# Two layers of grouped-query decode attention: a limit of four loads in flight

## The chip, the cores and the metric

The kernel runs on one core of a Trainium2 chip. The metric is the device time of one execution in microseconds (us). Before the change it is 1258.97 us, the median of three runs (1254.94 to 1260.19).

## What is computed

The input x is a batch of 8 single tokens of width 512. It goes twice through the same two blocks, with the same weights and the same caches: an attention block with 32 query heads, 8 key/value heads and 8192 cached positions of width 128, and a dense block of width 1792. Cut to what matters:

```
def attention(x, k_cache, v_cache, wq, wo):      # caches: 8 x 8 x 8192 x 128, bf16
    q = (x @ wq) as 32 heads of 128              # 4 query heads share one k/v head
    scores = q . k * 128**-0.5
    o = softmax(scores) . v
    return o @ wo

def dense(x, w1, w2):
    return silu(x @ w1) @ w2

x = x + attention(layernorm(x), k_cache, v_cache, wq, wo)
x = x + dense(layernorm(x), w1, w2)
x = x + attention(layernorm(x), k_cache, v_cache, wq, wo)
x = x + dense(layernorm(x), w1, w2)
```

The caches hold 128 MiB each, and nothing that large stays on the core, so most of them is read twice, once for each layer.

## The kernel before

**Tiles.** A task is one layer, one batch element and one key/value head; there are 2 x 8 x 8 = 128. The K and the V of a task are each cut into four granules of 2048 positions, 512 KB, 128 partitions of 4 KB. A granule is one load and fills one slot of an SBUF arena; there are 27 slots (`NSLOT`). For each task PE transposes K in groups of eight blocks of 128 x 128 (`emit_t`, L390 to L407: matmuls against an identity into the PSUM bank TPp, copied back over the K granule by DVE, or by ACT for three of eight). It then makes the scores (`emit_s`, L421 to L437, bank SCp), and fourteen groups later the product with V (`emit_pv`, L468 to L483, bank OTp). In between stand the softmax's maximum, exponential and sum (L442 to L466, on DVE, ACT and POOL).

**Order of the tasks.** The K granules of the last 18 of 32 places of a batch element (`KEEP`) stay transposed in the arena from layer 0 to layer 1, so that they are loaded once; for these layer 1 loads only V. While they are held, 9 slots are left for the stream. `make_tasks` (L136) therefore puts, for each batch element, the kept tasks of layer 0, then tasks that load both K and V, and then the kept tasks of layer 1; beside them runs the chain from layer 0's attention to layer 1's queries (projection, residual, layer norm, dense block: `block_stages`, `query`, lines 495 to 638, matmuls L547 and L565). This repeats for the eight batch elements.

**The loads.** `plan_loads` (L167) sorts all 880 granule loads by the position at which they are needed, and gives each a slot and the position after which it is free. All loads are issued from SP's queue, by the helper `dma` (L313), in that one order; SP does nothing else but issue loads, and at the end the output. The first entries are x (8 KB), four K granules, wq (4 MB), more granules until the 27 slots are taken, then wo (4 MB), w1 and w2 (1.8 MB each). Every slot has a semaphore of its own (`slsem`), which a load raises by 16 when it has landed in full; the weights and x have theirs. Before SP issues a load into a slot it waits for those who last used the slot: PE's, DVE's and ACT's semaphores (`acquire`, L88, and `wait`, L79, which emits a wait at L85 only if this engine has not yet waited for as much). Nothing else holds a load back in the program. Other engines wait for a load only when they use it.

**Waits.** `op` (L304) does the same for every instruction of the engines, so that a group of eight matmuls (`mm_group`, L322) waits once, ahead of its first, and has no wait inside.

Of the kernel before, what the change touches and what calls it, by code (L numbers as in the profile page):

```python
# [26 lines left out]
CW = 32  # L27
SETTLE = 2
ACT_EVAC = (1, 4, 7)

BF16 = mybir.dt.bfloat16
FP32 = mybir.dt.float32
# [156 lines left out]
def bass_interleave_layers__gqa_block_cached__dense_activation_silu__decode_kernel(  # L189
    nc: bass.Bass,  # L190
    A_x: bass.AP,
    A_k_cache: bass.AP,
    A_v_cache: bass.AP,
    A_wq: bass.AP,
    A_wo: bass.AP,
    B_x: bass.AP,
    B_w1: bass.AP,
    B_w2: bass.AP,
    out: bass.AP,
):  # L200
    with ExitStack() as ctx:
        _build(ctx, nc, A_x, A_k_cache, A_v_cache, A_wq, A_wo, B_w1, B_w2, out)


def _build(ctx, nc, A_x, A_k_cache, A_v_cache, A_wq, A_wo, B_w1, B_w2, out):
# [43 lines left out]
    def half(slot, h):  # L249
        o = slot * SLOT + h * GRP * 128  # L250
        return ARENA[:, o:o + GRP * 128]
# [37 lines left out]
    syn = Sync(nc, ctx)  # L289
# [6 lines left out]
    def res(name):  # L296
        if name not in R:
            R[name] = Res(name)
        return R[name]

    def r_half(slot, h):
        return res(f"slot{slot}_{h}")

    def op(eng, inst_fn, reads=(), writes=()):  # L304
        reads = [res(n) if isinstance(n, str) else n for n in reads]
        writes = [res(n) if isinstance(n, str) else n for n in writes]
        syn.acquire(eng, reads, writes)
        inst = inst_fn()
        tok = syn.mark(inst, eng)
        syn.release(tok, reads, writes)  # L310
        return tok

    def dma(eng, out_ap, in_ap, counter, reads=(), writes=()):  # L313
        reads = [res(n) if isinstance(n, str) else n for n in reads]
        writes = [res(n) if isinstance(n, str) else n for n in writes]
        syn.acquire(eng, reads, writes)
        tok = counter.next_tok()
        eng.dma_start(out_ap, in_ap).then_inc(counter.sem, 16)  # L318
        syn.release(tok, reads, writes)
        return tok  # L320

    def mm_group(steps, reads=(), writes=()):  # L322
# [13 lines left out]
    def issue(d):  # L336
        cache = A_k_cache if d.kind == "K" else A_v_cache
        src = cache[d.b, d.g].rearrange("(k p c) d -> k p (c d)", k=NGRAN, p=128)[d.k]
        dst = ARENA[:, d.slot * SLOT:(d.slot + 1) * SLOT]
        dma(sp, dst, src, slsem[d.slot], writes=[r_half(d.slot, 0), r_half(d.slot, 1)])  # L340
        (k_slot if d.kind == "K" else v_slot)[(d.b, d.g, d.k)] = d.slot

    with nc.Block() as block:

        @block.sync
        def _(sync_eng):
            dma(sp, Xr[0:B, :], x_in, wsem["x"], writes=["Xr"])

            op(pool, lambda: pool.memset(ident[:, :], 1.0), writes=["ident"])
# [14 lines left out]
            def load_wq():  # L364
                dma(sp, wq_sb[:, :, :], A_wq.rearrange("(kt p) n -> p kt n", p=128), wsem["wq"], writes=["wq"])
# [24 lines left out]
            def emit_t(i):  # L390
# [12 lines left out]
                dst = half(slot, h)  # L403
                if n % 8 in ACT_EVAC:
                    op(act, lambda: act.copy(dst, TPp[tb][:, :]), reads=[f"TP{tb}"], writes=[r_half(slot, h)])  # L405
# [359 lines left out]
```

## Time and profile before

| | |
|---|---|
| median of three runs | 1258.97 us |
| the profiled execution | 1258.23 us, its span 1256.5 us |
| mean granted TensorE clock | 0.934 |
| bytes moved by DMA | 477.16 MB, mean 380 GB/s |
| PE matmuls | 935.6 us busy, 74% |
| V loads, issue to landing | 512 of 512 KB, median 10.3 us |
| K loads, issue to landing | 368 of 512 KB, median 12.0 us |

A profile describes one execution. The span runs from the first to the last instruction; the time is a little longer. "Busy" counts an engine's instructions; issues and waits of a queue are not busy. PE, PEld, DVE, ACT and POOL are engines, SPq is the queue from which the loads are issued, L433 is line 433 of the kernel. A wait row names who waited, for whom, and then us in total, number of times and the longest; "issue" there means that the engine waited for nothing that the profile shows. GB/s in the page is given for 40 equal slices of the span. In-flight counts in the text are loads that have been issued and have not landed, taken from the records of issues and landings in the trace.

### The profile page before, as it was taken

To read this page: it belongs to the slowest core of one execution; us is meant where nothing else is said; L and a number is where in the kernel's file an instruction comes from. 1 tells how busy PE (TensorE), PEld (TensorE's weight loads), DVE (VectorE), ACT (ScalarE), POOL (GpSimd) and SP (SyncE) were. 2 spreads that over 40 slices of the span, in tenths; PEclk is the share of its full clock that TensorE was granted. 3 is DMA by queue.
4 is the path that set the end of the run, shared out by engine and by line. 5 is a ranking of instruction groups with operands and counts; after the bars stand their busy time and mean duration, and the time that the engine had idled before them with its cause. 6 is when DMAs were issued, how large, how long until landed. Compare 5 with 4: busy or idle time off the path is not lost. (4 is left out here: it accounts for less than half of the span.)

```text
span 1256.5 us, 57306 instructions
## 1 busy us (share of the span) xinstructions
PE 935.6 (74%) x25592; PEld 905.4 (72%) x25592; DVE 459.9 (37%) x1334; ACT 480.8 (38%) x1310; POOL 117.7 (9%) x298
## 2 busy tenths in 40 slices
PE   3687777777777767888778776888678777777775
PEld 3677776777677767777777776877677777777775
DVE  2333441445234432444144432434134432344422
ACT  1344433444244433444344433443344433543431
POOL 0000111001100011001100111011100111000010
PEclk9889998999899998999898999899899988999986
DMA  9999999999999999999999999999999999999993
GB/s 372 385 398 407 388 362 408 407 394 375 372 407 389 398 349 408 407 360 366 396 408 366 392 332 407 408 363 367 389 408 367 396 355 407 407 395 354 380 408 134
DMA packets 133973, 477.16 MB, mean 380 GB/s; under 512 B 14160, under 2 KB 20064, under 8 KB 133216
## 3 DMA queue, kind: packets, MB, share of 16 engines
q1 hardware_dynamic: 133728, 473.51, 96.5%
q8 instruction: 201, 3.29, 1.1%
q14 instruction: 44, 0.36, 0.1%
HBM read 473.44 MB, written 0.01 MB: 377 GB/s over the span
## 5 line engine op out<-in xcount | busy, mean ns | idle before, releaser
L399 PE MATMUL TPp<-ident,arena 128*128 128x128 bf16 x5888 | 476.9, 226 | 123.7 <-DMA arena<-in_A_k_cache_dram 60.7
L407 DVE COPY arena<-TPp 128x1024 bf16<-128x1024 bf16 x460 | 317.2, 691 | 521.7 <-PE TPp L399 518.5
L433 PE MATMUL SCp<-QT,arena 128*128 128x48 bf16 x8192 | 407.5, 190 | 100.0 <-issue 98.5
L405 ACT COPY arena<-TPp 128x1024 bf16<-128x1024 bf16 x276 | 278.9, 1011 | 523.1 <-PE TPp L399 523.0
L399 PEld LDWEIGHTS TPp<-ident,arena 128*128 128x128 bf16 x5888 | 356.2, 101 | 135.2 <-DMA arena<-in_A_k_cache_dram 71.6
L478 PE MATMUL OTp<-PT,arena 128*128 128x48 bf16 x8192 | 390.7, 187 | 52.2 <-issue 43.0
L433 PEld LDWEIGHTS SCp<-QT,arena 128*128 128x128 bf16 x8192 | 330.4, 100 | 115.3 <-issue 113.5
L478 PEld LDWEIGHTS OTp<-PT,arena 128*128 128x128 bf16 x8192 | 297.6, 99 | 55.0 <-issue 46.9
L454 ACT ACTIVATE PT<-SCp,nb 128x64 bf16<-128x64 f32 x512 | 161.1, 315 | 219.7 <-PE OTp L478 77.9
L446 POOL PARTITION_ALL_REDUCE mxa<-mx x128 | 47.5, 371 | 718.4 <-DVE mx L444 695.9
L454 ACT ACTIVATION_READ_ACCUMULATOR PT<-SCp,nb 128x1 f32 x512 | 99.0, 193 | 0.0
L461 POOL PARTITION_ALL_REDUCE ssa<-rs x128 | 55.2, 432 | 345.8 <-ACT PT L454 345.8
L492 DVE TENSOR_TENSOR at<-OTp,rcp 128x4 bf16<-128x4 f32 x128 | 20.7, 162 | 120.0 <-PE OTp L478 120.0
L444 DVE TENSOR_REDUCE mx<-SCp 128x4 f32<-128x256 f32 x128 | 52.6, 411 | 32.7 <-PE SCp L433 32.7
L565 PE MATMUL MISC<-at,wo 128*128 128x32 bf16 (+1 forms) x1152 | 39.5, 176 | 10.9 <-DMA wo<-in_A_wo_dram 5.5
L547 PE MATMUL MISC<-xnT,wq 128*128 128x32 bf16 (+1 forms) x1152 | 35.0, 177 | 8.5 <-issue 7.2
L565 PEld LDWEIGHTS MISC<-at,wo 128*128 128x128 bf16 x1152 | 33.9, 96 | 9.5 <-DMA wo<-in_A_wo_dram 5.6
L547 PEld LDWEIGHTS MISC<-xnT,wq 128*128 128x128 bf16 x1152 | 31.9, 96 | 9.2 <-issue 7.6
L451 DVE TENSOR_SCALAR nb<-mxa 128x4 f32<-128x4 f32 x128 | 21.4, 167 | 40.9 <-POOL mxa L446 40.9
L466 DVE RECIPROCAL rcp<-ssa 128x4 f32<-128x4 f32 x128 | 21.6, 169 | 7.6 <-POOL ssa L461 7.6
L547 PE MATMUL MISC<-hsT,w 128*128 128x32 bf16 (+1 forms) x504 | 16.3, 177 | 6.8 <-issue 4.9
L547 PE MATMUL MISC<-xnT,w 128*128 128x32 bf16 (+1 forms) x504 | 15.4, 176 | 6.5 <-DVE xnT L534 4.9
(34 smaller groups left out, 110.2 us busy)
## 6 DMA issues: line engine op xcount, KB each, us to landing
arena<-in_A_v_cache_dram SPq DMA_DIRECT2D x512, 512.0 KB, 10.3
arena<-in_A_k_cache_dram SPq DMA_DIRECT2D x368, 512.0 KB, 12.0
wq<-in_A_wq_dram SPq DMA_DIRECT2D x1, 4096.0 KB, 16.4
wo<-in_A_wo_dram SPq DMA_DIRECT2D x1, 4096.0 KB, 25.9
w<-in_B_w_dram SPq DMA_DIRECT2D x2, 1792.0 KB, 22.7
Xr<-in_A_x_dram SPq DMA_DIRECT2D x1, 8.0 KB
out_dram<-Xr SPq DMA_DIRECT2D x1, 8.0 KB
```

What stands on the lines that cost most here:

```text
L399: lambda c=c: pe.transpose(tpv[:, c, :], chunk(slot, h * GRP + c), ident[:, :])
L405: op(act, lambda: act.copy(dst, TPp[tb][:, :]), reads=[f"TP{tb}"], writes=[r_half(slot, h)])
L407: op(dve, lambda: dve.tensor_copy(dst, TPp[tb][:, :]), reads=[f"TP{tb}"], writes=[r_half(slot, h)])
L433: lambda c=c, cc=cc: pe.matmul(sc[:, :, cc:cc + RW], chunk(slot, h * GRP + c), qv, start=True, stop=True,)
L444: op(dve, lambda: dve.tensor_reduce(mx[st][:, :], scores(ti), AX.X, ALU.max), reads=[f"SC{ti % NSCP}"], writes=[f"mx{st}"])
L446: op(pool, lambda: pool.partition_all_reduce(mxa[st][:, :], mx[st][:, :], 128, bass.bass_isa.ReduceOp.max), reads=[f"mx{st}"], writes=[f"m ...
L454: op(act, lambda r=r: act.activation(PT[pb][:, r, :], scores(ti)[:, r, :], ACT.Exp, bias=nb[st][:, r:r + 1], scale=SM_SCALE, accum_out=rs[ ...
L461: op(pool, lambda: pool.partition_all_reduce(ssa[st][:, :], rs[st][:, :], 128, bass.bass_isa.ReduceOp.add), reads=[f"rs{st}"], writes=[f"s ...
L466: op(dve, lambda: dve.reciprocal(rcp[st][:, :], ssa[st][:, :]), reads=[f"ssa{st}"], writes=[f"rcp{st}"])
L478: lambda c=c, cc=cc: pe.matmul(otp, chunk(slot, h * GRP + c), PT[pb][:, :, cc:cc + 1].to_broadcast([128, REP, RW]), start=(cc == 0), stop= ...
L547: lambda o=o, k=k: pe.matmul(MISC[:, o * n:o * n + w], w_sb[:, k, o * 128:(o + 1) * 128], rhs_of(k).to_broadcast([128, w]) if n == 1 else ...
L565: lambda o=o, h=h: pe.matmul(MISC[:, o * w:(o + 1) * w], wo_sb[:, h, o * 128:(o + 1) * 128], rhs_of(h).to_broadcast([128, w]) if n == 1 el ...
```

## The change

The helper that issues loads keeps a list of the last four issued. When the list is full, SP first waits until the oldest of them has landed, and then goes on as before. The list holds x and the weights as well as the granules. The order of the loads, their slots and all other waits stay as they are; the output at the end does not go through the helper.

```diff
+FLIGHT = 4
...
+    flying = []
+
     def dma(eng, out_ap, in_ap, counter, reads=(), writes=()):
         reads = [res(n) if isinstance(n, str) else n for n in reads]
         writes = [res(n) if isinstance(n, str) else n for n in writes]
+        if len(flying) == FLIGHT:
+            syn.wait(eng, flying.pop(0))
         syn.acquire(eng, reads, writes)
         tok = counter.next_tok()
         eng.dma_start(out_ap, in_ap).then_inc(counter.sem, 16)
         syn.release(tok, reads, writes)
+        flying.append(tok)
         return tok
```

## The prediction

> **What bounds the kernel now.** I read the page first (busy shares, DMA rate by slice, the DMA queues), then the waits of PE and of SP, then PE's timeline around one idle gap, then windows of 20 us, and last the single records of DMA packets and landings in the trace.
>
> The page:
>
> ```profile
> PE 935.6 (74%) x25592; PEld 905.4 (72%) x25592; DVE 459.9 (37%) x1334; ACT 480.8 (38%) x1310; POOL 117.7 (9%) x298
> ...
> GB/s 372 385 398 407 388 362 408 407 394 375 372 407 389 398 349 408 407 360 366 396 408 366 392 332 407 408 363 367 389 408 367 396 355 407 407 395 354 380 408 134
> ...
> q1 hardware_dynamic: 133728, 473.51, 96.5%
> q8 instruction: 201, 3.29, 1.1%
> ```
>
> The reader is to see a load stream with a ceiling: many slices stand at 407 to 408 GB/s and none above. 477.16 MB at 407.5 GB/s would take 1171 us; the span is 1256.5. So DMA bounds the saturated slices and something else the others. Second, 201 packets on the instruction queue make 3.29 MB, 16 KB each; PE runs 2 x 25592 = 51184 instructions, about 255 a packet, so these packets are mainly PE's program.
>
> Waits over the whole span (us, times, longest):
>
> ```profile
> PE SCp L433 <- issue: 98.5, 63, 3.1
> PE TPp L399 <- DMA arena<-in_A_k_cache_dram: 60.7, 82, 2.1
> ...
> SPq L85 <- PE SCp L433: 263.1, 152, 5.1
> ...
> SPq L85 <- PE OTp L478: 199.3, 112, 5.0
> ```
>
> PE waits only some 66 us for loads. Its "issue" rows together (98.5 for SCp, 44.1 TPp, 43.0 OTp, 18.9 MISC) make 204.5 us in 138 stalls, 1.5 us each. SP in turn waits 462 us for PE to free a slot. So over long stretches PE sets the pace, and its largest loss is "issue". PE's timeline shows what that is:
>
> ```profile
> 329.53 0.37 PE L478 MATMUL OTp<-PT,arena 128*128 128x48 bf16 x8 [0.30 <-DMA arena<-in_A_v_cache_dram]
> 329.75 0.18 PE L433 MATMUL SCp<-QT,arena 128*128 128x48 bf16 x1
> 331.94 0.34 PE L433 MATMUL SCp<-QT,arena 128*128 128x48 bf16 x7 [2.00 <-issue]
> ```
>
> PE stops inside a group of eight matmuls, where the program has no wait, for 2.00 us. In the packet records a 16 KB instruction packet runs from 329.55 to 330.60, and PE goes on 1.34 us later. So do most of these stalls: of 131 longer than 0.3 us, 125 end 1.2 to 1.6 us after such a packet. The packets come some 6.2 us apart. PE waits for its own program, which comes through the same 16 DMA engines as the loads.
>
> Then I took each stall that follows such a stall, and counted from the earlier resumption (a block has begun, room for the next is free) to the start of the next instruction packet. By loads in flight: 1.3 us with two (5 cases), 1.9 with three (7), 2.6 with four (18), 3.7 with five (25), 3.75 with six or more (90), median each. The fetch waits behind loads already queued at its DMA engine, up to a limit near six loads.
>
> Windows (busy us of PE, PEld, DVE, ACT, POOL; clock; DMA share; GB/s):
>
> ```profile
> 300.00:320.00 20.00, 16.09 (x464) 15.83 (x461) 8.21 (x31) 6.53 (x13) 1.61 (x4) 0.91 0.87 325
> 320.00:340.00 20.00, 14.84 (x483) 14.32 (x479) 4.64 (x18) 6.09 (x28) 2.77 (x7) 0.91 0.99 386
> 340.00:360.00 20.00, 13.25 (x420) 12.83 (x415) 5.19 (x14) 7.51 (x27) 2.03 (x5) 1.00 1.03 408
> 360.00:380.00 20.00, 16.45 (x412) 16.14 (x407) 8.90 (x20) 9.43 (x24) 1.60 (x4) 0.91 1.03 407
> 380.00:400.00 20.00, 15.00 (x379) 14.73 (x380) 7.46 (x16) 8.29 (x22) 1.60 (x4) 0.91 1.03 407
> 400.00:420.00 20.00, 14.74 (x398) 14.13 (x395) 8.23 (x18) 9.59 (x23) 1.60 (x4) 1.00 0.96 364
> ```
>
> From 330 to 385 us twelve loads are in flight, DMA is full, and PE waits for no load: its waits there are "issue" alone (15.4 us). It falls behind the loads until the slots run out: from 385 to 410 SP waits 18.6 us for slots, and the rate drops to 364. This recurs for each of the eight batches.
>
> **The change, part by part.**
>
> *The order of the loads* stays. SP issues nothing else until the output, so behind a waiting issue stand only later loads.
>
> *The added wait, as it bears on the loads.* Three loads remain queued when the fourth last lands. In saturation loads land 1.28 us apart, so the slowest DMA engine still has 3 x 1.27 = 3.8 us of work. A fresh load reaches the engines sooner: the one issued at 319.27 us, with little queued, had its first packets at 320.24 (0.97 us), and the 8 KB load of x landed 1.45 us after its issue. With 0.1 us for SP to wake (estimate) that is about 1.5 us, under 3.8, so the slowest engine never runs dry; a load lands when the slowest is done. What is lost is the lead of the others, now at most 3.8 - 1.5 = 2.3 us; the spread from first to last engine of a landing reaches 4.6 us in the deep stretches today. Cost: nothing, or at worst this lost lead in each of eight deep stretches, 8 x 2.3 = 18 us. I take 4, near the lower end, since a landing goes by the slowest engine. Nothing is starved at the start either: the fourth K load waits for x (landed at 2.3 us), and the weights count as one load each but are 1.8 to 4 MB.
>
> *SP's extra instructions* (some 880 waits, partly instead of older ones): SP issues a load in 0.42 us when it may (302.37, 302.79) and needs one per 1.28. Nothing; their cover is that gap of 0.86 us.
>
> *The added wait, as it bears on PE's fetches.* With at most four loads in flight the fetch waits 2.6 us instead of 3.75, 1.1 less. 128 packets start with six or more loads in flight, and 162 us of stall follow them; taking from each stall 1.1 us or all of it gives 104 us of PE time, and at five loads some 19 more. Bounds: nothing (full engines keep the wait at 3.75) and all 204 us. I take 2.6, the row of that very depth.
>
> *What this is worth.* Once PE keeps up, the loads are late next: DMA is the floor. Over the 20 us windows from 80 to 1220 us I sum 20 x (1 - rate / 407.5): 59 us are lost below the ceiling. 22 of them lie just behind the deep stretches (windows at 260, 400, 540, 680, 820, 960, 1100, 1160), where PE has fallen behind; 104 / 8 = 13 us regained per stretch is far over the 2.7 lost, so I take all 22 (bounds 0 and 22). 37 lie at the hand-over between batches (as 300 to 320), where PE is busy 16.1 of 20 us and three to five loads are in flight already; there a third goes, 12 (bounds 0 and 37). In the tail from 1206 us four stalls of 1.5 to 2.7 us fall at seven to twelve loads; 4 us. Sum: 22 + 12 + 4 = 38 gained, 4 lost.
>
> By the Trainium skill, "DMA: Bandwidth & Descriptors", section "Queues, rings and completion order", a DMA engine takes turns between its queues packet by packet. By that rule a fetch waits for one load packet (0.16 us in this trace) however many are queued, and the sum would be 4 lost and none gained. The rows from 1.3 to 3.75 us by depth speak against it. The skill's "Runtime: NRT & Kernel Launch", section "Instruction fetch mechanics", gives blocks of 16 KiB, as here, and calls their cost mostly hidden; the trace has 204.5 us of it in the open.
>
> **The rivals.**
>
> *No change.* The fetch's wait is set by whether its DMA engine is busy, and with four loads all are: the four-load row comes partly from stretches with idle engines (from 1.1 to 4.5 us). Then PE is as late as before: 1258, or within 6 of it. For it: engines stay full at four. Against it: five busy loads give 3.7 but four give 2.6. The first rule named above would end here too. Chance 0.19.
>
> *Slower: four loads do not cover the way from a landing to the next load's packets.* It decides from 3.8 us on. Loads issued with three others in flight took 5.7 us (median of 65), over 4 that is 1.42 us a load against 1.28. Applied to the 695 loads that today go out with five or more in flight: 695 x 0.14 = 97, 1355 at its full price; if only some landings are late, 1265 to 1300. Against it: 1.5 us measured, and those 65 went out in stretches that lacked slots, where lagging engines make the 5.7. Chance 0.15.
>
> *Larger gain.* The hand-over is shortened as fully as the rest: 22 + 37 + 4 = 63, 1195. Against it: PE's own work fills most of it. Chance 0.08.
>
> *The wait is empty* (never more than four in flight) is excluded: landings take 10.3 and 12.0 us at the median, eight or nine loads deep.
>
> **How the numbers follow.** The profiled execution took 1258.2 us (span 1256.5, 1.7 around it): 1258.2 - 38 + 4 = 1224. The median of the three runs, 1259.0, is 0.8 above it, less than the sum's own rounding. The forecast, 1203 to 1252, has 0.58; its own range is that. A measurement can tell about 0.5% here, 6 us. Faster 0.58 + 0.08 = 0.66, same 0.19, slower 0.15. The range 1200 to 1275 leaves out some 0.06 below and 0.12 above.
>
> **What would show it.** Median landing near 5 us instead of 10 to 12. PE's "issue" waits near 100 us instead of 204.5, and instruction packets some 5 us apart. More PE waits for K loads. The dips after the deep stretches (400 to 420) gone, SP's waits for slots replaced by waits for landings. It is wrong if slices that now stand at 407 GB/s fall below 400, or if "issue" stays near 200.

## The result, and the profile after

The kernel with the limit takes 1332.58 us (median of four runs, 1330.72 to 1340.33) against 1259.58 for the kernel before on the same chip. The ratio is 1.0598, 95% interval 1.0548 to 1.0648: 73 us slower, where 34 us faster was forecast. The profiled execution took 1333.17 us, its span 1331.4. One execution is left out of the medians and ratios below, a slow one of the kernel with ten half loads: it took 1869 us at a granted clock of 0.791, where the three others took 1805 to 1828 at 0.807 to 0.815.

The page of the changed kernel: GB/s by slice, the queues, the chain of waits and the issues.

```profile
GB/s 369 377 362 384 357 366 364 356 367 365 340 360 384 382 357 349 362 364 360 356 358 343 378 347 357 375 356 374 364 364 358 369 387 356 351 365 360 347 350 195
...
q1 hardware_dynamic: 133728, 473.51, 95.7%
q8 instruction: 201, 3.29, 0.9%
...
DMA 93%; PE 4%; issue 1%; SPq 1%; DVE 0%; POOLq 0%; POOL 0%; ACT 0%; DVEq 0%
...
arena<-in_A_v_cache_dram SPq DMA_DIRECT2D x512, 512.0 KB, 5.7
arena<-in_A_k_cache_dram SPq DMA_DIRECT2D x368, 512.0 KB, 5.7
```

The reader is to see that no slice reaches the 407 to 408 GB/s that a third of the slices had before: the highest is 387, most lie near 360. The chain of waits is now 93% DMA. A load lands after 5.7 us instead of 10 to 12, so the limit does what it says.

The waits, PE's and then SP's (us, times, longest):

```profile
PE TPp L405 <- DMA arena<-in_A_k_cache_dram: 221.8, 248, 2.6
...
PE SCp L439 <- issue: 47.4, 34, 4.2
...
PE OTp L484 <- DMA arena<-in_A_v_cache_dram: 29.7, 65, 1.2
PE OTp L484 <- issue: 19.8, 14, 3.0
```

```profile
SPq L323 <- DMA arena<-in_A_v_cache_dram: 494.3, 499, 2.6
SPq L323 <- DMA arena<-in_A_k_cache_dram: 373.4, 356, 2.8
SPq L86 <- PE SCp L439: 28.0, 29, 3.2
```

PE's "issue" waits are down from 204.5 to 79.5 us in all, but its waits for loads are up from 71 to 262. SP waited 462 us for slots; now it waits 868 for landings and some 34 for slots. The windows that stood at 408 and 407 GB/s now read:

```profile
340.00:360.00 20.00, 14.36 (x458) 13.97 (x456) 2.73 (x12) 6.39 (x29) 2.41 (x6) 0.83 0.96 344
360.00:380.00 20.00, 14.30 (x390) 13.55 (x387) 5.14 (x13) 7.16 (x25) 2.03 (x5) 0.91 0.95 359
380.00:400.00 20.00, 16.04 (x355) 15.57 (x352) 7.74 (x18) 7.57 (x19) 1.17 (x3) 0.83 0.95 346
```

From the landing records: 71% of the loads after 80 us land within 1.35 us of the load before them (1.258 us on average). The others come up to 3.2 us after the load before, 1.8 at the median. Now take from each of these gaps 1.284 us, the pace of the loads alone (measured below). What is left over is the delay of the loads; it is 148 us in all in the changed kernel, against 71 us in the kernel before. Set against the starts of the instruction packets, 132 of the 148 us fall 2 to 4 us behind such a start, and 54 of the 71 before: 78 us more, just there, where the kernel lost 73. In every other microsecond behind a start the delay in the changed kernel is 0.05 us a load or less.

### The profile page after: what moved, and what is told of

Read it like the earlier page. It is cut to its first block, busy times and chain, and to the rows that moved or that the text cites. A ratio compares the mean times of both kernels' runs of the same rounds, so it can differ in the third digit from the quotient of the medians.

```text
span 1331.4 us, 57557 instructions
## 1 busy us (share of the span) xinstructions
PE 953.2 (72%) x25592; PEld 907.8 (68%) x25592; DVE 460.6 (35%) x1334; ACT 480.0 (36%) x1310; POOL 117.7 (9%) x298
## 4 chain that ended last, share of the span: by engine, by line
DMA 93%; PE 4%; issue 1%; SPq 1%; DVE 0%; POOLq 0%; POOL 0%; ACT 0%; DVEq 0%
DMA arena<-in_A_v_cache_dram 48%; DMA arena<-in_A_k_cache_dram 45%; PE TPp L405 1%; PE MISC L553 1%; DMA w<-in_B_w_dram 1%; SPq L323 1%; PE SCp L439 1%; PE OTp L484 1%; DVE eh L607 0%; DVE Xr L739 0%; PE MISC L732 0%; PE MISC L571 0%; DVE tr L535 0%; DVE tr L536 0%; DVE yr L538 0%
## 5 line engine op out<-in xcount | busy, mean ns | idle before, releaser
L439 PE MATMUL SCp<-QT,arena 128*128 128x48 bf16 x8192 | 398.4, 189 | 48.9 <-issue 47.4
L484 PE MATMUL OTp<-PT,arena 128*128 128x48 bf16 x8192 | 384.2, 186 | 51.5 <-DMA arena<-in_A_v_cache_dram 29.7
L439 PEld LDWEIGHTS SCp<-QT,arena 128*128 128x128 bf16 x8192 | 324.8, 99 | 56.6 <-issue 55.0
L484 PEld LDWEIGHTS OTp<-PT,arena 128*128 128x128 bf16 x8192 | 291.8, 98 | 58.6 <-DMA arena<-in_A_v_cache_dram 39.4
```

The lines of the kernel that those rows point to most:

```text
L439: lambda c=c, cc=cc: pe.matmul(sc[:, :, cc:cc + RW], chunk(slot, h * GRP + c), qv, start=True, stop=True,)
L484: lambda c=c, cc=cc: pe.matmul(otp, chunk(slot, h * GRP + c), PT[pb][:, :, cc:cc + 1].to_broadcast([128, REP, RW]), start=(cc == 0), stop= ...
```

## The experiments

Two theories. **A:** four loads cover the way from a landing to the next load, but each 16 KB instruction packet makes one DMA engine late, and with only four loads the others do not stay far enough ahead to cover that; so each packet sets the whole stream back. **B** (the slower rival of the prediction): the way of 5.7 us is itself too long for four loads.

### Loads alone, with and without the limit

```diff
+    FILL = 0
...
+        if busy[0] and eng is not pe:
+            return None
...
     def mm_group(steps, reads=(), writes=()):
+        if not FILL:
+            return None
```

`busy[0]` is set after the setup. The edit is against the changed kernel. Each of the five runs in this section and the next two was executed once.

> Loads alone: every operation of PE, DVE, ACT and POOL after the setup is left out, so SP issues the same 884 loads with the limit of four and nothing waits for a slot but an earlier load; the output is x itself. Theory A (each 16 KB instruction packet sets the whole load stream back by about 0.9 us, and without such packets four loads cover the way): loads land 1.26 us apart, 880 of them and 12 MB of weights (23 loads' worth) take 903 x 1.26 = 1138 us, the kernel 1140 to 1160. Theory B (the way from a landing to the next load's landing, 5.8 us with three others in flight, is too long by itself): 880 x 1.47 + 23 x 1.26 = 1323, 1310 to 1340.

> Loads alone without a limit (every operation of PE, DVE, ACT and POOL after the setup left out; the output is x itself). Theory A: without instruction packets the limit of four costs nothing, so this takes what the loads alone took with it, 1160 to 1175. Theory B: 1140 to 1160, and the limit's cost is the difference.

1169.67 us with the limit, 1169.63 without it (there `FLIGHT` is 1000). The page of the run with the limit:

```profile
GB/s 366 388 394 410 409 410 409 410 409 410 398 410 409 409 408 407 409 410 410 410 410 396 408 409 410 409 410 410 410 409 410 410 402 406 410 409 410 409 408 369
```

Four loads in flight keep 410 GB/s: a load lands 1.284 us after the one before, 5.10 us after its issue (with four always in flight, this is just four times 1.28). The time is 10 us over what A expected, since I had used 1.258 us a load; B's 1310 to 1340 is out. The limit costs nothing on its own.

### PE's instruction packets put back, without any dependence

```diff
-            for f in steps:
-                inst = f()
+            for _f in steps[:: FILL]:
+                inst = pe.matmul(MISC[:, 0:48], ident[:, :], wide[:, 0:48], start=True, stop=True)
```

with `FILL = 1`.

> Loads with the limit of four, and beside them PE runs as many matmuls as the kernel has, in the same groups, but on two constant tiles, and waits for no load and no other engine. DVE, ACT and POOL are left out; the output is x itself. It puts the 200 instruction packets back without any dependence. Theory A: some 190 packets in the time of the stream, 0.9 us each, 1140 + 170 = 1310, or a little less if PE is done before the loads. Theory B: as without PE's work, 1310 to 1340, and equal to the run of the loads alone.

> Loads and PE's 25592 constant matmuls as in the run with the limit of four, but without a limit. The output is x itself. Theory A: with a deep queue each DMA engine bears its own packets only, 200 / 16 x 1.1 = 14 us, so 1140 + 14 = 1155 to 1180. Theory B: 1140 to 1160, since nothing waits for a landing.

With the limit 1304.5 us, as A has it. The rate by slice, with PE's busy share above it:

```profile
PE   7667666677666776676667766767767676200000
...
GB/s 360 365 367 367 355 380 353 357 358 370 341 330 367 365 344 361 380 353 367 358 365 363 367 362 360 356 370 361 356 364 364 367 358 355 374 408 409 410 406 371
```

PE shares no data and no semaphore with the loads here, and yet they run at 360 GB/s as long as it runs; when it is done, at 1120 us, they go back to 408 to 410. That it is the packets, and not PE's work as such, shows in where the delay lies: of 130 us after 80 us, 112 fall 2 to 4 us behind the start of an instruction packet. Without a limit, the same PE program leaves them at 407 to 409 in 22 of 40 slices:

```profile
PE   6666666666666666666666666666666666666669
...
GB/s 374 384 397 408 407 404 408 408 380 407 408 408 397 399 405 407 407 382 409 407 408 383 404 408 407 408 385 407 407 408 383 409 407 407 396 391 408 405 383 19
```

The landing records tell why the deep queue hides the packets. A load has landed when the last of the 16 DMA engines has finished its part; call the time by which the median engine was done earlier the load's lead. At the median of the loads the lead is 3.3 us without a limit and 1.1 us with four in flight. In the run of the loads alone with the limit it is 0.5 us.

The run without a limit took 1221 us, over the 1155 to 1180 expected, but not for its loads: the last landed at 1192 us, and PE went on to 1219. PE, which waits for no load and no other engine here, needs 1219 us beside a deep queue and 1120 beside four loads. First with the limit, then without (busy us, mean ns of one, idle us before):

```profile
L341 PE MATMUL MISC<-wide,ident 128*128 128x48 bf16 x25592 | 777.3, 192 | 343.3 <-issue 341.2
```

```profile
L341 PE MATMUL MISC<-wide,ident 128*128 128x48 bf16 x25592 | 804.9, 194 | 414.4 <-issue 411.9
```

Of the 99 us, 71 are "issue". The other 28 are the matmuls' own busy time, at a mean granted clock of 0.83 instead of 0.86 while PE ran. An instruction packet comes every 6.2 us in the one without a limit and every 5.6 us with it (medians). Of the stops over 0.3 us, 189 of 195 without a limit and 165 of 171 with it end 1.2 to 1.6 us behind the end of such a packet. From the end of a stop to the start of the next packet it is 3.7 us without a limit and 3.2 with it (medians).

### Fewer instruction packets

```diff
-    FILL = 1
+    FILL = 4
...
-                inst = pe.matmul(MISC[:, 0:48], ident[:, :], wide[:, 0:48], start=True, stop=True)
+                inst = pe.matmul(MISC[:, 0:320], ident[:, :], wide[:, 0:320], start=True, stop=True)
```

> As the run with PE's constant matmuls, but a quarter as many and each 320 columns wide, so that the instruction packets come some 20 us apart instead of 5 (about 50 in all). The output is x itself. Theory A: about 50 x 0.9 = 45 us over the loads alone, 1185. Theory B: no difference to the loads alone. The prediction's picture (one late DMA engine is covered by the others' lead of 2.3 us when packets are rare): no difference to the loads alone either, and loads alone at 1140.

1231.9 us, 62 over the loads alone; A expected 45, the prediction's picture nothing. Over the loads' own 1.284 us, landings are late by 58 us in all after 80 us, with 46 packets: 1.3 us each. In the run with all packets it is 130 us for 186 of them, 0.7 each; without a limit 24 us for 180, 0.14 each. So with four loads in flight a packet that comes alone costs the stream more than its own 1.0 us, and with a deep queue little. Of the 58 us, 44 fall 2 to 4 us behind a packet's start (0.96 us a packet, about what it lasts) and 13 come 8 to 15 us behind it. PE itself never stops here, with a packet only every 17 us:

```profile
L341 PE MATMUL MISC<-wide,ident 128*128 128x320 bf16 x6398 | 871.9, 300 | 1.9 <-POOL wide L373 1.9
```

The landing records of this run show why the other engines do not cover it. For each load: when it landed, how long after the load before, and its lead:

```
load 279   417.79   +1.41   0.60
                             an instruction packet starts at 418.57
load 280   420.60   +2.81   2.05
load 281   421.87   +1.26   2.05
load 282   423.10   +1.24   2.03
load 283   424.35   +1.25   2.04
load 284   425.60   +1.25   1.49
load 285   426.85   +1.24   1.15
load 286   428.34   +1.49   0.85
load 287   429.74   +1.40   0.74
```

One engine is late: in loads 280 to 283 the last of the 16 comes 1.7 us after the last but one (0.06 at the median in the run of loads alone). The stream slips by 1.5 us, and the median engine is 2 us ahead. That lead would cover much of the next packet. But it melts: over all loads until 870 us it is 2.0 us in the third microsecond behind a packet's start, 1.4 at 4 to 8 us, 0.9 at 10 to 12 and 0.6 from 14 us on. The reason is in the issues: load 284 goes out at 420.62, 0.02 us after load 280 has landed, so every engine, however far ahead, gets it only then, 1.5 us later than at the stream's own pace. With a deep queue the next loads are already there.

### The number of loads in flight

```diff
-FLIGHT = 4
+FLIGHT = 5
```

and the same with 3, 6 and 8.

> The changed kernel with three loads in flight. Theory A: two loads of 1.27 us stand queued at a landing, 2.5 us against a way of about 1.5, so an instruction packet is covered less still; 1430 to 1520. Theory B (5.8 us over the number in flight): 5.3 / 3 = 1.75 us a load or more, 1550 to 1650.

> The changed kernel with five loads in flight. Theory A: a lead of 3.6 us covers most instruction packets; 1265 to 1290. Theory B: 5.8 / 5 = 1.17 us a load is under the stream's own 1.26, so the limit costs nothing: 1255 to 1265.

> The changed kernel with six loads in flight. Theory A: nearly all packets covered, 1250 to 1268; PE's fetches wait 3.7 us as with twelve, so no gain from them. Theory B: 1255 to 1265.

> The changed kernel with eight loads in flight. Theory A and theory B: as before the change, 1253 to 1265.

> The changed kernel with five loads in flight once more, in more rounds, as the version that came out fastest. If its gain is real it lies again 0.6 to 1.3% under the kernel before (1247 to 1254 against 1262); if the first result was a chance of that chip, within 0.4%.

| loads in flight | us | ratio to before, 95% interval | PE "issue" waits | PE waits for loads |
|---|---|---|---|---|
| 3 | 1566.4 (one run) | | 3.9 | 497 |
| 4 | 1332.6 | 1.0598 (1.0548 to 1.0648) | 79.5 | 262 |
| 5 | 1252.0 | 0.9908 (0.9874 to 0.9942) | 155.4 | 125 |
| 5, again | 1248.9 | 0.9901 (0.9881 to 0.9921) | 160.0 | 112 |
| 6 | 1261.1 | 0.9987 (0.9963 to 1.0011) | 199.5 | 79 |
| 8 | 1260.5 | 0.9981 (0.9956 to 1.0005) | 207.3 | 76 |
| no limit | 1259.6 | 1 | 204.5 | 71 |

Each ratio is against the kernel before on the same chip (1259.6 to 1262.3 us), so compare the ratios. The two columns of waits are from one profiled execution each.

With three, B's range holds and A's does not: here the way is too long by itself, as B had it for four. Of the loads there, 289 had no instruction packet in their time (none started from 1 us before the issue to 1 us before the landing); they landed 4.7 us after their issue at the median, and 3 x 1.28 = 3.8 us does not cover that. All loads took 5.1 us at the median, and with three always in flight one lands every 1.73 us. Four loads, 5.1 us, leave about 0.5 us over 4.7, which agrees with the lead of 0.5 us in the run of the loads alone.

Six and eight are like no limit, as both theories have it. Five is faster than before by 1.0% in both runs, which neither expected. Its waits:

```profile
PE TPp L405 <- DMA arena<-in_A_k_cache_dram: 106.4, 162, 1.7
...
PE SCp L439 <- issue: 78.4, 54, 3.0
...
PE OTp L484 <- issue: 34.4, 31, 2.4
```

PE has 49 us less of "issue" than before and waits 53 us more for loads, more often but more briefly, while the loads are still at 395 to 407 GB/s in most slices. SP's waits for slots fell from 462 to 210 us. PE's fetches are hardly quicker: from the end of a stop to the next packet it is 3.6 us with five and 3.7 before. Of the 10 to 12 us gained, 7 to 9 are landings that are less late (64 and 62 us in all instead of 71), and 2 come behind the last landing (16.5 us instead of 18.5). Why they are less late I have not taken apart.

### Half loads

The question was whether what counts is the lead or simply the bytes in flight. First each granule was cut by partitions, with a semaphore for each half:

```diff
+        for u in range(2):
+            rows = slice(64 * u, 64 * u + 64)
+            dma(sp, ARENA[rows, d.slot * SLOT:(d.slot + 1) * SLOT], src[rows], slsem[d.slot][u],
+                writes=[r_half(d.slot, 0, u), r_half(d.slot, 1, u)])
```

> Each granule in two loads of 64 partitions, with a semaphore each, and a limit of eight such half loads: the same 2 MB in flight, but the next half is let go when a half has landed. Theory A in its refined form (a DMA engine that must wait for the next load takes some 4.6 us from a load's issue until it has landed on all 16, and what four loads' 5.1 us leave over, 0.5 us, is all the lead that can cover an instruction packet): with halves the way is 4.6 - 0.6 = 4.0 us and 1.1 us are left over, so 1260 to 1305. If only the bytes in flight count: 1320 to 1340, as with four whole loads.

> Half loads as before, nine in flight (4.5 loads' worth). Theory A refined: 9 x 0.635 - 4.0 = 1.7 us left over, as much as five whole loads have (6.35 - 4.6), and PE's fetches wait a little less: 1240 to 1258. If only the bytes count: midway between four and five loads, 1280 to 1300.

> Half loads, ten in flight (five loads' worth). Theory A refined: 2.3 us left over, fetches as with five whole loads: 1240 to 1255. If only the bytes count: 1248 to 1256, as with five whole loads.

1881, 1818 and 1810 us (ratios 1.497, 1.446 and 1.439). All lie far outside the expectations, and they tell nothing of the question, since loads of 64 partitions were slow in themselves. In the run with nine the DMA engines are busy throughout, at 265 GB/s:

```profile
DMA packets 148064, 477.32 MB, mean 265 GB/s; under 512 B 28240, under 2 KB 34144, under 8 KB 147296
...
q1 hardware_dynamic: 147808, 473.56, 100.5%
```

Then each granule was cut by columns, all 128 partitions, 2 KB each:

```diff
+        for h in range(2):
+            dma(sp, half(d.slot, h), src[:, h * GRP * 128:(h + 1) * GRP * 128], slsem[d.slot][h],
+                writes=[r_half(d.slot, h)])
```

> Each granule in two loads by columns (128 partitions of 2 KB each, all DMA engines and partitions as with whole granules), each with its own semaphore and waited for by the group of eight blocks that uses it; no limit. It is the control of the next three. If 2 KB packets cost nothing: 1250 to 1265, perhaps a little faster since PE can start on the first half. If each packet has a price: slower by it.

> Halves by columns, eight in flight, 2 MB as with four whole loads. Theory A refined (what the loads in flight leave over beyond the way of a waiting DMA engine covers the instruction packets: 8 x 0.64 = 5.1 us less 4.6 - 0.6 = 4.0 leaves 1.1, against 0.5 with four whole loads and 1.75 with five): 1260 to 1305. If the bytes in flight alone decide: 1320 to 1340.

> Halves by columns, nine in flight. Theory A refined: 1.7 us left over, as with five whole loads, 1240 to 1258. If the bytes alone decide: 1280 to 1300.

> Halves by columns, ten in flight. Theory A refined: 2.3 us left over and fetches as with five whole loads, 1240 to 1255. If the bytes alone decide: 1246 to 1256.

The control without a limit takes 1315.7 us, ratio 1.0423 (1.0397 to 1.0449): cutting the loads costs 53 us, and the slices at the ceiling stand at 386 GB/s instead of 407. So the absolute expectations miss by that, and each limit is to be compared with the control. Eight halves, 2 MB in flight like the four whole loads: 1314.8, ratio 1.0399, no dearer than the control, where four whole loads cost 73 us. Nine: 1301.0, some 15 us under the control; ten: 1308.7, some 7 under, with intervals that overlap (1.0330 to 1.0408). None is faster than the kernel before. Bytes in flight alone would have made eight as dear as four whole loads; on this slower stream they are not. That fits the lead theory, but does not show it: the slower stream helps too (eight halves last 8 x 0.68 = 5.4 us instead of 5.1), and I have not taken that apart.

## Why the prediction was wrong

- **The step that failed: "The added wait, as it bears on the loads", priced at 4 us, at most 18.** The runs showed some 77 us there: landings late by 148 us in the changed kernel against 71 before, the whole of the difference 2 to 4 us behind the starts of instruction packets. The sum had no term for what these packets do to the loads. It saw them only as something that PE waits for, and not as something that makes one of the loads' own DMA engines late, each of some 194 times, though it says itself that they come through the same engines. The bound of 18 us was wrong in kind for the same reason: it counted one lost lead in each of eight deep stretches.
- **Why it seemed covered.** The lead of 2.3 us was 3.8 less 1.5, with 1.5 taken from a load's first packets and from an 8 KB load, so it stopped where the data begins. The end of the way is when the load has landed on all 16 engines. The very load that gave the 0.97 us, issued at 319.27, landed 3.44 us after its issue; the first load of all, with only x in flight, took 3.5. With the others in flight the way is 4.7 us (the run with three), and four loads last 5.1, so 0.5 us is left, half of what a packet lasts. "The slowest engine never runs dry" holds as far as the landings tell: without a packet, four loads in flight cost nothing (1169.67 against 1169.63 us).
- **What bounds the kernel.** That PE waits for its own program, and longer beside a deep queue, is right: its stops in the runs with the constant matmuls make 412 us beside a deep queue and 341 beside four loads, with nothing else for it to wait for.
- **PE's fetches.** Those 71 us are two thirds of the 104 forecast. The single term was too large: the wait from a resumption to the next packet is 3.3 us at the median in the changed kernel and 3.2 with the constant matmuls, against 3.7 deep, so 0.4 to 0.5 us less and not 1.1. The 2.6 came from a row of 18 cases, partly from stretches with idle engines, as the first rival said. The sign "near 100" for PE's "issue" waits came out (79.5), but in part for another reason: "issue" falls wherever PE waits for loads instead, down to 3.9 us with three loads in flight. Another sign failed: the packets come 6.2 us apart as before, not 5. And the sign named for being wrong came, slices at 407 falling below 400.
- **"What this is worth", 38 us.** SP waits some 34 us for slots instead of 462, so that part of the picture came true. But with the stream itself slower nothing of it was seen in the time.
- **The rivals.** The slower case had 0.15. Its price, 97 us in full, came near the 73, but by luck: with four loads the way is covered as long as no instruction packet comes. Its row of 5.7 us was set aside because lagging engines make it. They do (the median engine was done 1.5 us before the last), but that was no reason to set it aside: lagging engines are just what the limit makes dear. Whether packets made them lag in that row is not shown: 61 of its 65 loads had a packet in their time, and the other four took no less.
- **No change** was out by its time, but its reason, that full engines keep PE's fetches nearly as late at four, was closer than the forecast: 3.2 to 3.3 us against 3.7. What part of the fall in "issue" is quicker fetching can't be told in the changed kernel.
- **The Trainium skill.** By the packet-by-packet turns of the Trainium skill's "DMA: Bandwidth & Descriptors", section "Queues, rings and completion order", the depth would not matter to a fetch; the 412 and 341 us of stops disagree. The prediction also read that rule too small: a packet in that section of the Trainium skill is typically some 9 to 17 descriptors, and the 0.16 us taken for it is one 4 KB record of the trace. By the Trainium skill's "Runtime: NRT & Kernel Launch", section "Instruction fetch mechanics", fetches are mostly hidden. In this kernel they are not: PE's 204.5 us of "issue" lie in the open, and with four loads in flight the loads pay too. In the run with a packet only every 17 us PE did not stop, as the Trainium skill has it.

What stays open: the records do not name a packet's DMA engine, so the late engine of the landings could not be matched with the packet itself; they are tied by time alone. Nor is it shown why packets 17 us apart cost 1.3 us each and packets some 6 us apart 0.7; a lead that has not yet melted would do it.

## What to carry to other kernels

A limit on loads in flight must be sized by the time from a load's issue until it has landed on every DMA engine, not by its first packet, and must leave room for one engine to be made late by something else, here an instruction packet of 1.0 us. Before counting on a depth, look at who else uses the DMA engines: with four in flight, loads alone ran at 410 GB/s, and at 360 beside a PE whose only tie to them was the fetching of its program. When an engine stops in the middle of a group without a wait, look for its instruction packets. A slightly shorter queue can still be worth trying (five here, 1.0% faster than none), but four cost 6.0%, so try the neighbours too.

## What the runs showed of the hardware that was not expected

- Beside a PE that runs constant matmuls, a stream of loads falls from 410 to 360 GB/s when four loads are in flight, and hardly when the queue is deep (407 to 409 in 22 of 40 slices); the delay lies 2 to 4 us behind the starts of PE's 16 KB instruction packets.
- A PE program of 25592 small matmuls that waits for nothing stopped for 412 us beside a deep load queue and for 341 us beside four loads; nearly all of the stops end 1.2 to 1.6 us behind an instruction packet.
- Loads of 64 partitions by 4 KB moved 265 GB/s with the DMA engines busy throughout, against 407 to 408 in the full slices with 128 partitions by 4 KB; 128 partitions by 2 KB reached 386.
